# Later output products and spread v groups in the attention steps of a four-layer kernel

## The chip, the core and the metric

The kernel runs on one core of one Trainium2 chip. A core has TensorE (PE) for matrix products, VectorE (DVE), ScalarE (ACT) and GpSimd (POOL) for the rest, SyncE (SP), which here only issues transfers, and 16 DMA engines that carry the transfers. Each engine works through its own list of instructions in order and waits on semaphores for the others. The metric is the device time of one launch in microseconds (us), the median of several runs.

## What is computed

Two blocks are applied in turn, A, B, A, B, each behind a layer norm and added to its input x (2048 tokens of 576 channels; bf16 inputs, output within the tolerance of the reference).

```python
def _A_ref(x, wqkv, wo):            # attention: 32 heads of 18 channels
    W, dil = (8, 2)                 # each token looks at itself and 7 earlier ones, 2 apart
    q, k, v = ...                   # x @ wqkv
    ...
    logits = jnp.einsum('bhsd,bhswd->bhsw', q, kg) * scale
    attn = _softmax(logits, axis=-1)
    o = jnp.einsum('bhsw,bhswd->bhsd', attn, vg)
    return o @ wo

def _B_ref(x, w_in, w_sp, b_sp, w_out):   # gated MLP, 2304 + 2304 channels
    z = _gelu(jnp.einsum('bsd,df->bsf', x, w_in))
    z1, z2 = z[..., :Fh], _layernorm(z[..., Fh:])
    g = jnp.einsum('ts,bsf->btf', w_sp, z2) + b_sp[None, :, None]
    return jnp.einsum('bsf,fd->bsd', z1 * g, w_out)

x = x + _A_ref(_layernorm(x), A_wqkv, A_wo)
x = x + _B_ref(_layernorm(x), ...)
x = x + _A_ref(_layernorm(x), A_wqkv, A_wo)
x = x + _B_ref(_layernorm(x), ...)
```

## The kernel before

The change touches only `layer_A`, which is built twice: with `li == 0` (the first attention) and with `li == 2` (the second). The order of its instructions on every engine is written out by hand and kept as written.

The 2048 tokens are cut into two halves and each half into nine query tiles of 114 tokens (the last of a half has 112), `NT = 18` tiles t. A tile reads the keys and values of its own tokens and of the 14 before them, so 128 rows. Every tile takes two steps, s = 2t and s = 2t + 1, each for 16 of the 32 heads; there are `NST = 36` steps. Rows of the residual stream are handled in blocks of 128 tokens, i = 0 to 15.

A step issues, in this order: the score products of the next step (`L_mm`, line 444, into two large PSUM tiles of tag H) and their exponentials (`EXP`, line 453, on ScalarE, into one of four P buffers); then its own products with v (`PV`, line 464, TensorE), which VectorE normalises into the tile's buffer o_t (lines 470 and 471; there are three o_t buffers, so tile t + 3 overwrites tile t's). After the second step of a tile SP issues a transposing DMA from o_t to one of three slots (line 474). Then come the functions that a table holds for this step:

- `PG` (line 409): a group of q or k columns for 512 tokens, five products; VectorE evacuates it to a staging buffer (line 378), and SP and POOL issue transfers from there to the packed q/k tile QK. The groups of the second token half run inside the steps.
- `VW` (line 386): half of the v columns for one tile, five products, evacuated by VectorE or ScalarE into `v_ext`.
- `O_CP` (line 483): VectorE copies a transposed tile from its slot into a ring `oT` of five row blocks.
- `WO(i, hh)` (line 509): half of the output columns of row block i, five products from `oT`; VectorE adds the residual input `xo` (line 512) into `x_new`.
- `XO(i)`: SP loads the residual input of row blocks i and i + 1 (288 KB in the first attention).
- `LN_STATS(i)` on VectorE, then `LN_XN(i)` on POOL, the layer norm for the MLP that follows; `XST(i)`, SP's store of the new residual; `LN_T(i)`, SP's transposing DMA of the normalised block into `xnT`.
- `O_T`: the last two tiles are transposed on TensorE (line 489) instead of by DMA.
- `load_win2a`, `win2b_piece`: POOL issues loads of the MLP's weights.

`PV`, `PG`, `VW`, `WO` and `O_T` all take their PSUM tile from one set of four (tag PT), in turn. Transfers from SP are issued one after the other; each waits for its data to be ready before the next is issued.

Before the change, the step of `WO(i, 0)` follows from the tile t that completes row block i (`row_step`): 2t + 6 or 2t + 5, at the end 2t + 4 and 2t + 3; the second half runs one step later, so from step 8 on (first attention) or 7 on (second) there is about one half a step, with a gap in the middle, where the first token half ends, and two halves in step 32. The v groups of the second token half run from step 18 to 33 in the first attention, two steps for each tile.

After the steps the MLP follows. Its first products (line 815) are mixed with the last output products by the scheduler; the first thing it does on ScalarE after the gelus (line 829) is a square (line 833).

Of the kernel before, what the change touches and what calls it, by code (L numbers as in the profile page):

```python
# [18 lines left out]
P = 128  # L19
# [46 lines left out]
class K:  # L66
# [258 lines left out]
    def layer_A(self, li):  # L325
        nc, tc, cfg = self.nc, self.tc, self.cfg
        S, NT, XW, NS = cfg.S, cfg.NT, cfg.XW, cfg.NS
# [31 lines left out]
        def tdim(t):  # L359
            nq = cfg.tiles[t][1]  # L360
            return HALO + nq, nq

        def q0_(t):
            return cfg.tiles[t][0]
# [67 lines left out]
        NST = 2 * NT  # L432
# [101 lines left out]
        if li == 0:  # L534
# [114 lines left out]
            nvw0, nvw = 4, 9  # L649
        else:  # L650
# [12 lines left out]
            nvw0, nvw = 0, 4  # L663
# [14 lines left out]
        def at(s, f, *a):  # L678
            table.setdefault(s, []).append((f, a))
        pgs = [(d, qk, cc) for d, cc in ((0, 2), (1, 2), (2, 2), (0, 3), (1, 3), (2, 3), (3, 2), (3, 3), (4, 2), (4, 3))  # L680
               for qk in ((1, 0) if d < 4 else (0,))]
        PG_END = 14
        pre, pgs = pgs[:6], pgs[6:]
        for k_, (d, qk, cc) in enumerate(pgs):
            at(1 + k_ if li == 0 else (k_ * PG_END) // len(pgs), PG, d, qk, cc, True)
        for t in range(nvw, NT):
            for hh in range(2):
                if li == 0 and t == nvw:
                    at(13 * hh, VW, t, hh, True)
                else:  # L690
                    at(2 * t - 2 + hh, VW, t, hh, 2 * t - 2 + hh >= PG_END and hh == 0)
        row_step = {}
        for i in range(NS):
            t = next(t_ for t_ in range(NT) if q0_(t_) + tdim(t_)[1] >= (i + 1) * P)
            row_step[i] = 2 * t + (6 if li == 0 and t < 10 else 5 if t < NT - 4 else 4 if t < NT - 2 else 3)
        for t in range(NT - 2):
            if t < NT - 4:
                at(2 * t + (5 if li == 0 and t < 10 else 4), O_CP, t)
        for i in range(NS):
            s = row_step[i]  # L700
            if i % 2 == 0:
                at(max(s - 5, row_step[i - 3] + 1) if i >= 4 else s - 5, XO, i)
            at(s, WO, i, 0)
            at(s + 1, WO, i, 1)
            at(s + 1, LN_STATS, i)
            at(s + 2, LN_XN, i)
            at(s + 2, XST, i)
            if i < NS - 1:
                at(max(s + 4, 24 + (5 * i) // 4) if li == 0 else s + 4, LN_T, i)
        for t in range(NT - 4, NT - 2):  # L710
            at(2 * t + 3, O_CP, t)
        if li == 0:
            at(0, self.load_wo, nc.sync)
            for f in reversed(self.load_win2a(nc.gpsimd)):
# [368 lines left out]
```

## Time and profile before

| | |
|---|---|
| median of 3 runs | 1185.18 us (1184.57 to 1185.57) |
| the profiled execution | 1188.89 us, of which the profiled span is 1187.1 us |
| mean granted TensorE clock | 0.999 |

Busy time of the engines by stage, from the profile's windows (us; clock is the share of TensorE's full clock that was granted):

| stage | length | PE | DVE | ACT | POOL | clock |
|---|---|---|---|---|---|---|
| before the steps, first attention (0 to 41) | 41 | 38.28 | 33.91 | 20.31 | 24.01 | 1.00 |
| its steps 0 to 7 (41 to 64) | 23 | 22.30 | 16.93 | 17.53 | 13.54 | 1.00 |
| steps 8 to 13 (64 to 84) | 20 | 16.73 | 13.64 | 10.57 | 9.27 | 0.91 |
| steps 14 to 17 (84 to 92) | 8 | 7.52 | 7.01 | 6.98 | 7.62 | 1.00 |
| steps 18 to 33 (92 to 128) | 36 | 35.17 | 32.38 | 31.07 | 29.33 | 1.00 |
| last steps (128 to 135) | 7 | 6.44 | 6.20 | 3.39 | 6.04 | 1.00 |
| first MLP (135 to 620) | 485 | 481.81 | 200.82 | 118.95 | 77.77 | 1.00 |
| second attention and its MLP's start (620 to 760) | 140 | 136.52 | 101.98 | 103.78 | 96.54 | 1.00 |
| second MLP (760 to 1187) | 427 | 421.52 | 142.02 | 64.68 | 23.46 | 1.00 |

How to read the views shown below: the timeline gives the start of a merged run of instructions, its length, the engine, the line of the kernel, what it writes and reads, and in brackets how long the engine sat idle just before and whose event ended that. A list of waits gives the engine and line that waited, who ended the wait, the total, the count and the longest. A window gives its length, the busy time of PE, its weight loads, DVE, ACT and POOL (with counts), then the granted clock, the DMA share and GB/s. Matrix products are pipelined, so their shown lengths overlap; distances from start to start are used for their cost.

### The profile page before, as it was taken

How to read it: one execution, taken by the hardware profiler on the slowest of the kernel's cores; microseconds unless marked ns; L12 is line 12 of the kernel's file. 1: busy time of each engine (PE TensorE's matmuls, PEld its weight loads, DVE VectorE, ACT ScalarE, POOL GpSimd, SP SyncE). 2: the span in 40 equal slices, each digit the busy share in tenths (PEclk: the TensorE clock that was granted, in tenths of full speed). 3: DMA queues.
4: the chain of work that ended last, by engine and by line, in shares of the span. 5: the costliest groups of instructions: out<-in, count | busy, mean ns of one | idle time of the engine just before them, and what ended most of it. 6: DMA issues, size and time to landing. Idle time of an engine off the chain costs nothing. (4 is left out here: it accounts for less than half of the span.)

```text
span 1187.1 us, 20409 instructions
## 1 busy us (share of the span) xinstructions
PE 1166.3 (98%) x8307; PEld 622.3 (52%) x8406; DVE 554.9 (47%) x1232; ACT 377.3 (32%) x621; POOL 287.6 (24%) x383
## 2 busy tenths in 40 slices
PE   9989999999999999999999999999999999999998
PEld 5557544444444444457755774444444444444676
DVE  8778687332233232245556886863232233232321
ACT  5568677211100111102156786770111110111000
POOL 4758784100000000001143867840000000000000
PEclk9999999999999999999999999999999999999999
DMA  8989994000000000049656998900000000001332
GB/s 196 201 154 208 180 198 100 23 12 12 12 1 12 12 12 1 15 139 284 169 100 115 206 226 173 238 14 10 12 12 12 12 1 12 12 1 38 115 105 73
DMA packets 179478, 101.57 MB, mean 86 GB/s; under 512 B 135711, under 2 KB 160735, under 8 KB 179384
## 3 DMA queue, kind: packets, MB, share of 16 engines
q1 hardware_dynamic: 166520, 78.50, 31.3%
q0 software_dynamic: 6512, 16.00, 5.4%
q10 hardware_dynamic: 6352, 5.75, 1.6%
q8 instruction: 66, 1.08, 0.4%
q14 instruction: 28, 0.23, 0.1%
HBM read 42.39 MB, written 16.53 MB: 50 GB/s over the span
## 5 line engine op out<-in xcount | busy, mean ns | idle before, releaser
L929 PE MATMUL pg<-Wq,Z 128*128 128x512 bf16 x2258 | 497.8, 379 | 2.5
L929 PEld LDWEIGHTS <-Z 128*128 128x128 bf16 x2304 | 225.4, 98 | 271.8
L933 DVE TENSOR_TENSOR g_tmp<-pg,ln_xn 128x512 f32<-128x512 f32 x144 | 99.6, 692 | 422.5 <-PE pg L929 422.5
L924 ACT ACTIVATE z1T<-pz 128x1024 bf16<-128x1024 f32 x36 | 34.9, 1021 | 497.4 <-PE pz L905 493.8
L80 POOL DMA_DIRECT2D wout<-in_B_w_out_dram x4 | 4.3, 1065 | 600.8 <-PE pg L929 600.8
L971 PE MATMUL po<-wout,Z 128*128 128x288 bf16 x1152 | 141.4, 286 | 0.0
L453 ACT ACTIVATE P_sb<-L_ps 128x912 bf16<-128x912 f32 (+1 forms) x144 | 125.8, 929 | 42.3 <-PE L_ps L444 41.8
L971 PEld LDWEIGHTS <-Z 128*128 128x128 bf16 x1152 | 112.7, 98 | 28.8
L815 PEld LDWEIGHTS <-xnT 128*128 128x128 bf16 (+1 forms) x800 | 66.5, 97 | 83.7 <-issue 26.5
L815 PE MATMUL pz<-win2a,xnT 128*128 128x512 bf16 x380 | 103.9, 380 | 2.3 <-ACT zp L829 1.4
L934 DVE TENSOR_TENSOR Z<-g_tmp,z1T 128x512 bf16<-128x512 f32 x144 | 99.7, 692 | 12.6 <-DVE g_tmp L933 0.5
L905 PEld LDWEIGHTS <-w 128*128 128x128 bf16 (+1 forms) x640 | 53.7, 97 | 74.0 <-issue 13.6
L409 PE MATMUL pp<-xnT,wqk_sb 128*128 128x512 bf16 x341 | 82.3, 382 | 2.1 <-DVE o_t L471 0.6
L829 ACT ACTIVATE zp<-pz 128x1024 bf16<-128x1024 f32 x64 | 65.5, 1023 | 36.0 <-PE pz L815 16.9
L981 DVE TENSOR_TENSOR x_new<-po,xo 128x288 f32<-128x288 f32 (+1 forms) x64 | 28.8, 456 | 87.7 <-PE po L971 83.6
L905 PE MATMUL pz<-xnT,w 128*128 128x512 bf16 (+1 forms) x314 | 66.2, 380 | 0.3
L905 PE MATMUL pz1s<-xnT,w 128*128 128x512 bf16 (+1 forms) x312 | 65.3, 379 | 0.7 <-issue 0.6
L831 DVE CUSTOM_DVE_ANT_0 Z<-zp 128x1536 bf16<-128x1536 bf16 x32 | 56.8, 1774 | 12.5 <-ACT zp L829 7.6
L815 PE MATMUL pz<-win2b,xnT 64*128 64x512 bf16 (+1 forms) x240 | 59.7, 380 | 0.0
L80 POOL DMA_DIRECT2D QK<-stg x81 | 50.7, 631 | 35.6 <-DVE stg L378 18.7
L245 POOL TENSOR_SCALAR ln_xn<-x_new,ln_mv,ln_rstd 128x576 bf16<-128x576 f32 x23 | 53.0, 2306 | 2.0
L386 PE MATMUL pv<-wv_sb,xnT 128*128 128x288 bf16 (+1 forms) x360 | 52.8, 286 | 0.6 <-DVE o_t L471 0.5
(118 smaller groups left out, 1007.1 us busy)
## 6 DMA issues: line engine op xcount, KB each, us to landing
xres<-x_new SPq DMA_DIRECT2D x48, 288.0 KB
xo<-xres SPq DMA_DIRECT2D x32, 288.0 KB
wout<-in_B_w_out_dram POOLq DMA_DIRECT2D x4, 1296.0 KB, 8.6
xo<-xres SPq DMA_DIRECT2D x8, 576.0 KB
w<-in_B_w_in_dram SPq DMA_DIRECT2D x16, 256.0 KB
QK<-stg POOLq DMA_DIRECT2D x53, 72.0 KB, 4.7
QK<-stg SPq DMA_DIRECT2D x41, 72.0 KB
xo<-in_A_x_dram SPq DMA_DIRECT2D x8, 288.0 KB
```

The lines of the kernel that those rows point to most:

```text
L80: return eng.dma_start(out=out, in_=in_)
L245: e.tensor_scalar(out=xn[:nrows, 0:D], in0=x_t[:nrows, :], scalar1=mv[:nrows, 0:1], scalar2=rstd[:nrows, 0:1], op0=ALU.subtract, op1=ALU.mult)
L409: nc.tensor.matmul(pp[:, :], lhsT=w, rhs=self.xnT[:, c, PADL + cc * 512:PADL + (cc + 1) * 512], start=(c == 0), stop=(c == 4))
L453: nc.scalar.activation(out=P_bufs[(2 * s + jp) % 4][:nk, :, :, 0:nq], in_=Lv[:nk, :, :, 0:nq], func=ACT.Exp, scale=scale)
L815: nc.tensor.matmul(pzvs[ci][:, sub * 512:sub * 512 + w], lhsT=self.xnT[r0:r1, c, PADL + i * P:PADL + (i + 1) * P], rhs=win2(c)[r0:r1, c0 + ...
L829: nc.scalar.activation(out=zp[:, c0:c0 + cn], in_=pzvs[ci][:, 0:cn], func=ACT.Gelu_apprx_tanh, accum_out=sums[:, ci:ci + 1])
L831: nc.vector.tensor_tensor_reduce(out=spare[:, 0:SQ_D], in0=zp[:, 0:SQ_D], in1=zp[:, 0:SQ_D], scale=1.0, scalar=0.0, op0=ALU.mult, op1=ALU. ...
L905: nc.tensor.matmul(outs[a_], lhsT=w1[r0:r1, c, sub * P:(sub + 1) * P], rhs=self.xnT[r0:r1, c, PADL + q * 512:PADL + (q + 1) * 512], start= ...
L929: nc.tensor.matmul(pg[:, :], lhsT=Z[:, jj, i, sub * P:(sub + 1) * P], rhs=Wq[q][:, i, :], start=(i == 0), stop=(i == NS - 1))
L933: nc.vector.tensor_tensor(out=tmp[:], in0=pg[:, :], in1=bsp[:, qs], op=ALU.add)
L934: nc.vector.tensor_tensor(out=uT(jj)[:, sub, qs], in0=tmp[:], in1=z1Ts[jj, sub][:, qs], op=ALU.mult)
L971: nc.tensor.matmul(acc[hh], lhsT=uT(j // 2)[:, j % 2, i * P:(i + 1) * P], rhs=wouts[j // NJH][:, j % NJH, hh * 288:(hh + 1) * 288], start= ...
```

## The change

The table is filled by other rules. The output products get a hand-written list of steps, `wo_steps`. In the first attention row block i < 8 has its halves in steps 10 + 2i and 11 + 2i, then (26, 27), (28, 29), (30, 30), (31, 32), (33, 34), (34, 35), (35, 36), (37, 38). In the second it is 9 + 2i and 10 + 2i, then (25, 26), (27, 28), (29, 30), (31, 32), (33, 34), (34, 35), (35, 36), (37, 38). So the halves of the first row blocks run two steps later than before, those from block 8 on at the same step or one later, and step 32 has one half in place of two.

What hangs on a row block moves with it: `XO` (five steps before the first half), `LN_STATS`, `LN_XN`, `XST` and `LN_T`. `O_CP(t)` moves to step 2t + 6 at the latest (before: 2t + 5 for t < 10 in the first attention, else 2t + 4), or to the step before its row block's product. In the first attention the v groups of the second token half (tiles 10 to 17) spread over steps 14 to 32, four in five steps, in place of one in each of the steps 18 to 33; in the second they stay.

The built order on the engines shows it: on TensorE the products of line 509 leave the steps 8 and 9 and the v products stand in steps 14 to 17; on SP the first `XO` goes from before the q/k transfers of the second staging buffer to behind the transposing DMA of tile 2.

```diff
-        for t in range(nvw, NT):
-            for hh in range(2):
-                if li == 0 and t == nvw:
-                    at(13 * hh, VW, t, hh, True)
-                else:
-                    at(2 * t - 2 + hh, VW, t, hh, 2 * t - 2 + hh >= PG_END and hh == 0)
-        row_step = {}
+        vws = [(t, hh) for t in range(nvw, NT) for hh in range(2)]
+        if li == 0:
+            at(0, VW, *vws[0], True)
+            at(13, VW, *vws[1], True)
+            vws = vws[2:]
+        for k_, (t, hh) in enumerate(vws):
+            s = PG_END + (5 * k_) // 4 if li == 0 else 2 * t - 2 + hh
+            at(s, VW, t, hh, s >= PG_END and hh == 0)
+        lag = 10 if li == 0 else 9
+        wo_steps = [(lag + 2 * i, lag + 2 * i + 1) for i in range(8)]
+        wo_steps += ([(26, 27), (28, 29), (30, 30), (31, 32), (33, 34), (34, 35)] if li == 0 else
+                     [(25, 26), (27, 28), (29, 30), (31, 32), (33, 34), (34, 35)]) + [(NST - 1, NST), (NST + 1, NST + 2)]
+        for t in range(NT - 2):
+            s = wo_steps[q0_(t) // P][0] - 1
+            if t < NT - 3:
+                at(min(2 * t + 6, s), O_CP, t)
         for i in range(NS):
-            t = next(t_ for t_ in range(NT) if q0_(t_) + tdim(t_)[1] >= (i + 1) * P)
-            row_step[i] = 2 * t + (6 if li == 0 and t < 10 else 5 if t < NT - 4 else 4 if t < NT - 2 else 3)
-        for t in range(NT - 2):
-            if t < NT - 4:
-                at(2 * t + (5 if li == 0 and t < 10 else 4), O_CP, t)
-        for i in range(NS):
-            s = row_step[i]
+            s, s1 = wo_steps[i]
             if i % 2 == 0:
-                at(max(s - 5, row_step[i - 3] + 1) if i >= 4 else s - 5, XO, i)
+                at(max(s - 5, wo_steps[i - 3][1]) if i >= 4 else s - 5, XO, i)
             at(s, WO, i, 0)
-            at(s + 1, WO, i, 1)
-            at(s + 1, LN_STATS, i)
-            at(s + 2, LN_XN, i)
-            at(s + 2, XST, i)
+            at(s1, WO, i, 1)
+            at(s1, LN_STATS, i)
+            at(s1 + 1, LN_XN, i)
+            at(s1 + 1, XST, i)
             if i < NS - 1:
-                at(max(s + 4, 24 + (5 * i) // 4) if li == 0 else s + 4, LN_T, i)
-        for t in range(NT - 4, NT - 2):
-            at(2 * t + 3, O_CP, t)
+                at(max(s1 + 3, 24 + (5 * i) // 4) if li == 0 else s1 + 3, LN_T, i)
+        at(2 * (NT - 3) + 3, O_CP, NT - 3)
```

## The prediction

> **What bounds the kernel now.** I read the page first, then TensorE's waits in the two attentions, then the timelines of TensorE and VectorE step by step, then the granted clock by window. The page says who sets the time:
>
> ```profile
> PE 1166.3 (98%) x8307; PEld 622.3 (52%) x8406; DVE 554.9 (47%) x1232; ACT 377.3 (32%) x621; POOL 287.6 (24%) x383
> ```
>
> TensorE is busy for 98% of the span, so a reordering can win only what TensorE stands idle or runs slowly: 1187.1 - 1166.3 = 20.8 us of idle time, plus time at a lowered clock. TensorE's waits from 64 to 130 us (the first attention's steps 8 to 34), with total, count and longest:
>
> ```profile
> PE pw L509 <- DVE oT L483: 2.9, 2, 2.4
> PE L_ps L444 <- ACT P_sb L453: 0.9, 3, 0.4
> PE pp L409 <- DVE o_t L471: 0.6, 1, 0.6
> ```
>
> Most of it is one wait of an output product (L509) for VectorE's copy of a transposed tile into oT (L483). TensorE's timeline around it (start, us, what; in brackets the idle time before it):
>
> ```profile
> 69.48 0.57 PE L464 MATMUL O_ps<-v_ext,P_sb 128*128 128x19 bf16 x16
> 69.90 1.24 PE L409 MATMUL pp<-xnT,wqk_sb 128*128 128x512 bf16 x5
> 73.58 0.79 PE L509 MATMUL pw<-wo_sb,oT 128*128 128x288 bf16 x5 [2.45 <-DVE oT L483]
> ...
> 74.63 0.57 PE L464 MATMUL O_ps<-v_ext,P_sb 128*128 128x19 bf16 x16
> 75.75 0.61 PE L409 MATMUL pp<-xnT,wqk_sb 128*128 128x512 bf16 x1 [0.56 <-DVE o_t L471]
> 76.58 1.49 PE L409 MATMUL pp<-xnT,wqk_sb 128*128 128x512 bf16 x3 [0.22 <-issue]
> 77.86 1.32 PE L509 MATMUL pw<-wo_sb,oT 128*128 128x288 bf16 x5
> ...
> 79.45 0.57 PE L464 MATMUL O_ps<-v_ext,P_sb 128*128 128x19 bf16 x16
> ```
>
> Each step has one L464 group (PV), so the distance of two PV starts is a step's length. Step 9, whose PV starts at 66.94, takes 2.54 us. Steps 10 and 11, with the same work, take 5.15 and 4.82. VectorE shows the cause, and the granted clock shows a second loss:
>
> ```profile
> 68.64 0.69 DVE L378 CAST stg<-pp 128x512 bf16<-128x512 f32 x1 [0.26 <-PE pp L409]
> 73.19 0.34 DVE L483 COPY oT<-o_slot 128x570 bf16<-128x570 bf16 x1 [3.86 <-DMA o_slot<-o_t]
> ```
> ```profile
> 76.00:78.00 2.00, 1.78 (x5) 0.74 (x5) 1.28 (x4) 0.53 (x1) 1.41 (x3) 0.50 0.13 18
> ```
>
> The copy of tile 2 waits 3.86 us for its transposing DMA, issued on SP at 64.42. After the idle time TensorE runs at 0.50 of its clock (third number from the end), which the trace's clock record puts at 3.41 us long. The excess adds up: 2.45 + 0.56 + 0.22 idle, plus 3.41 / 2 = 1.71 lost at half clock, is 4.94; the two steps' excess over 2.53 each is 4.91.
>
> **The change, part by part.** Prices of TensorE's groups, from start to start: score products L 0.33 (64.08 to 64.41), PV 0.42, a q/k group (PG) 1.07, an output half (WO) 0.71, a v group (VW) 0.61 (92.17 to 92.78). Steps by kind, from PV starts: PG alone 2.09 (51.88 to 64.41 over six), PG+WO 2.53, WO alone 1.88 (84.24 to 91.75 over four), VW+WO 2.16 (91.75 to 104.72 over six). WO alone has 1.46 us of TensorE work in 1.88: there the exponentials (1.75 us of ScalarE a step) bind. No work is added or removed, so I sum step lengths.
>
> First attention, steps 8 to 34:
> - Steps 8 and 9 lose their output products: 2 x (2.09 - 2.53) = -0.88.
> - Steps 10 and 11 return to 2.53: -4.91, before what is left of the stall.
> - Steps 14 to 17 gain a v group: 4 x 2.16 against 7.51 measured: +1.13.
> - Steps 18, 23, 28 and 33 have none any more: 1.88 each against 2.17, 2.08, 2.25 and 2.28: -1.26.
> - Step 24 gains an output half (2.24 to 2.16), step 30 has two (2.25 to 2.78), step 32 one instead of two (2.78 to 2.16): -0.17.
> - Step 34 lasts 2.69 with 0.41 + 0.46 idle. The half that moves here needs no late tile and fills that: PV 0.42, two halves 1.42, transposes 0.25 make 2.09; two MLP matmuls (0.43) that stood there come later: -0.17.
>
> Sum -6.26. Against it stands what remains of the stall. The copy of tile 2 moves behind step 10, but the buffers of o_t number three: VectorE's write of o_t for tile 5, in step 10 too, overwrites what tile 2's transposing DMA reads, and waits for the same landing. So the wait on VectorE does not go; it starts later (about 68.9 us) and TensorE's cover grows. Behind it on VectorE queue the q/k evacuation, the copy and the first sum of step 10; TensorE waits for them through the four PSUM buffers of tag PT, first at step 11's q/k group, nominally 71.0 us. When the DMA lands therefore decides. In the trace 12 of its 16 increments came at 70.58 to 71.72, the last four at 73.12 to 73.16. Ahead of it on SP stood the first residual load (XO, 288 KB; its 256 packets fill 63 to 66 us). The change puts that load behind it, with SP issuing the transpose some 0.5 us earlier. I take the landing 2.2 us earlier, near 71.0: VectorE is free at 71.4, TensorE stalls 0.4 us, and VectorE's backlog (2.03 us of work a step in steps 13 to 19 against 2.16) costs perhaps 0.4 more: 0.8 in all. Bounds: 0 (landing at 70.5) and, with the landing unmoved, 2.6 us idle plus 1.71 at half clock.
>
> Where the stall goes, what is late next? The last q/k columns (d = 4) are evacuated at step 12, about 77.6 us, and issued by SP until 81.1; POOL's moves of this kind land in a median of 4.9 us, so near 86; step 18 reads them near 86.7. No wait, within 1 us. The residual load now lands near 72.5, when VectorE is about there. At the end SP is busy almost without a gap from 117.7 to 144.6, row 12's sums come a step later, and the first square of the MLP waits 2.45 us for a transpose, which costs TensorE 0.88: I give back 0.5 (0 to 1). First attention: -6.26 + 0.8 + 0.5 = -5.0.
>
> Second attention, the same output products, its v groups unmoved:
>
> ```profile
> 686.56 0.57 PE L464 MATMUL O_ps<-v_ext,P_sb 128*128 128x19 bf16 x16
> ...
> 688.67 0.56 PE L464 MATMUL O_ps<-v_ext,P_sb 128*128 128x19 bf16 x16
> ...
> 690.62 0.56 PE L464 MATMUL O_ps<-v_ext,P_sb 128*128 128x19 bf16 x16
> ...
> 713.16 0.79 PE L509 MATMUL pw<-wo_sb,oT 128*128 128x288 bf16 x5 [0.48 <-DVE oT L483]
> ```
>
> Steps 23 and 24 have no output product, yet last 2.11 and 1.95 us with 1.36 us of work: two free places, filled by the change (+0.05 and +0.21). They come from steps 7 and 8, where PG, VW and WO together are TensorE's own 3.15 us; without WO 2.43, above ScalarE's 1.75 + 0.41: -1.44. Step 32 loses its second half (2.77 to 2.16): -0.61. Step 34 (here 0.42 + 0.48 idle) as above: -0.2. Sum -2.0; the row tail on POOL (about 3.1 us a row, back to back at the end) gives back 0.4 (0 to 0.8): -1.6. The moved residual loads, stores and transposes keep their distance in steps to what reads them, and SP's own waits in this attention are for VectorE and POOL.
>
> Total -6.6. Against the profiled execution's own span: 1187.1 to 1180.5, and its time of 1188.89 lies 1.79 outside the span. That execution is 3.71 above the median of 1185.18; the difference is applied to the median: 1178.6.
>
> The trace has half clock after 2.45 and 0.56 us of idle time with work between. The Trainium skill, "TensorE: Matmul & The Clock Gate", section "What's actually happening", says that the clock halves after an idle window of about 3.4 us; read so, neither gap would have done it, and the 1.71 would not belong to the stall, for a total of -4.9 and 1180.3. The measured half clock decides here.
>
> The residual load is moved behind the transpose, yet the trace shows POOL's q/k moves on the same transfer engines at that time. The Trainium skill, "DMA: Bandwidth & Descriptors", section "Issuing engines are not separate DMA queues", says that transfers interleave on the same 16 engines whoever started them; that speaks against the earlier landing, and with an unmoved landing the sum is that of the second case below.
>
> **The rivals.**
> 1. *Forecast*: as above. Its own range: nothing given back and a small 0.5 us further is -8.8, 1176.4; 2.0 of stall and both tails at their full price is -6.26 + 2.0 + 1.0 - 2.0 + 0.8 = -4.5, 1180.7.
> 2. *The transpose lands at 73.2 as before*, since the last four increments came 1.4 us after the twelfth and may have nothing to do with the load. Then 4.3 replaces 0.8: -6.6 + 3.5 = -3.1, 1182.1. For it: the o_t write waits for it just the same. Against: a 288 KB load leaves its front.
> 3. *The end holds the MLP*: SP's queue, nearly full from 117.7, does not come earlier, the square waits as late as before, and the first attention's gain becomes its wait. Only the second's 1.6 stays: 1183.6. Against: before 105 us SP has room, and its transposes are tied to steps.
> 4. *Slower*: the transpose of tile 3, now behind the residual load and four q/k moves, holds VectorE in step 12 (o_t of tile 6 waits for it). TensorE's cover ends near 77.1 us; each microsecond later costs one, and the half clock 1.71. It eats the whole gain when it lands after 77.1 + 6.6 - 1.7 = 82.0, and is slower by 0.2% from 84.4 on; at 85.5, 1188.7 - 1185.2 = 3.5 slower. Against: it landed at 73.9 before, 4.5 us after its issue, and the slowest in that stretch took 8.7.
>
> That the instructions do not move is excluded: the built order shows the output products gone from steps 8 and 9 and the v groups in 14 to 17.
>
> **How the numbers follow.** About 0.2% (2.4 us) is what a measurement of this kernel tells from no change. Chances: forecast 0.68, landing unmoved 0.19, held end 0.06, slower 0.04, a gain beyond 8.8 us 0.03. The second case straddles 1182.8: four fifths of it is faster. Faster 0.68 + 0.15 + 0.03 = 0.86; same 0.04 + 0.06 = 0.10; slower 0.04. The time is the forecast's, 1178.6; the range 1176.4 to 1182.6 holds cases one and most of two, about 0.83.
>
> **What would show it.** Right: steps 8 and 9 at 2.1 us, steps 10 to 12 near 2.5 with under 1 us idle and a clock of 1.00; VectorE's wait at o_t (L471) instead of the copy, ending near 71; steps 14 to 17 near 2.16; no idle before L509 in step 34; in the second attention steps 7 and 8 at 2.4, 23 and 24 at 2.2. Wrong: a clock of 0.50 near 72 to 80, a wait of VectorE until 73, a longer idle time before the first gelus, or spread steps well above 2.16.

## The result, and the profile after

| | before | after |
|---|---|---|
| median | 1186.05 us (1183.72 to 1190.33, 22 runs) | 1183.52 us (1181.44 to 1187.09, 22 runs) |
| ratio of the times | | 0.9975, 95% interval 0.9966 to 0.9985 |
| the profiled execution, its span | 1188.89, 1187.1 us | 1182.29, 1180.5 us |

The medians differ by 2.5 us; the ratio is worth 3.0 us, with an interval of 1.8 to 4.0. Forecast were 6.6 us and 1178.6; the time is 0.9 us above the range. The two profiled executions do differ by the forecast 6.6 us. That agreement is chance, and the trap of this case: the profile of before is of an execution 2.8 us above the median of the 22.

The line of engines on the page of after, then TensorE's waits from 64 to 130 us (total, count, longest):

```profile
PE 1169.8 (99%) x8406; PEld 622.2 (53%) x8406; DVE 553.0 (47%) x1232; ACT 377.3 (32%) x621; POOL 285.8 (24%) x383
```
```profile
PE L_ps L444 <- ACT P_sb L453: 1.3, 4, 0.4
PE pv L386 <- DVE o_t L471: 1.0, 2, 0.7
PE pw L509 <- DVE x_new L512: 0.2, 1, 0.2
```

The 2.9 us at the output product are gone. TensorE's PV groups (the lines between them are left out) and one line of VectorE at the place of the old stall (start, length, engine and line; idle time and its end in brackets), then two windows (the clock is the third number from the end):

```profile
67.99 0.56 PE L464 MATMUL O_ps<-v_ext,P_sb 128*128 128x19 bf16 x16
70.52 0.57 PE L464 MATMUL O_ps<-v_ext,P_sb 128*128 128x19 bf16 x16
73.06 0.57 PE L464 MATMUL O_ps<-v_ext,P_sb 128*128 128x19 bf16 x16
75.59 0.57 PE L464 MATMUL O_ps<-v_ext,P_sb 128*128 128x19 bf16 x16
...
70.35 0.46 DVE L471 TENSOR_TENSOR o_t<-O_ps,rec 128x288 bf16<-128x288 f32 x1 [1.50 <-DMA o_slot<-o_t]
```
```profile
74.00:76.00 2.00, 2.00 (x41) 1.24 (x40) 1.90 (x8) 1.22 (x3) 0.58 (x1) 1.00 1.03 174
76.00:78.00 2.00, 2.00 (x39) 1.47 (x36) 1.97 (x8) 1.68 (x3) 1.63 (x4) 1.00 0.76 211
```

Steps 10 to 12 last 2.53 us each, at full clock. VectorE waits at the write of o_t instead of at the copy, until 70.35, and TensorE does not notice. This is the picture that the prediction drew. The first row blocks of the MLP tell another part, on ScalarE and TensorE:

```profile
137.61 0.84 ACT L835 ACTIVATE Z<-zp 128x768 bf16<-128x768 bf16 x1 [2.55 <-DMA xnT<-stg]
...
139.60 0.81 PE L817 MATMUL pz<-win2a,xnT 128*128 128x512 bf16 x3 [0.98 <-ACT zp L831]
```

The square waits 2.55 us for transposes out of the staging buffers, and TensorE loses 0.98 behind it. In the second attention the free places are filled, steps 23 and 24 (forecast 2.2 each; PV groups alone):

```profile
677.22 0.56 PE L464 MATMUL O_ps<-v_ext,P_sb 128*128 128x19 bf16 x16
679.33 0.56 PE L464 MATMUL O_ps<-v_ext,P_sb 128*128 128x19 bf16 x16
681.54 0.57 PE L464 MATMUL O_ps<-v_ext,P_sb 128*128 128x19 bf16 x16
```

### The profile page after: what moved, and what is told of

It reads as the page before. It is cut to its first block, busy times and chain, and to the rows that moved or that the text cites. A ratio compares the mean times of both kernels' runs of the same rounds, so it can differ in the third digit from the quotient of the medians.

```text
span 1180.5 us, 20534 instructions
## 1 busy us (share of the span) xinstructions
PE 1169.8 (99%) x8406; PEld 622.2 (53%) x8406; DVE 553.0 (47%) x1232; ACT 377.3 (32%) x621; POOL 285.8 (24%) x383
## 4 chain that ended last, share of the span: by engine, by line
PE 89%; POOL 4%; DMA 2%; DVE 2%; issue 1%; ACT 1%; SPq 0%; POOLq 0%; ACTq 0%; DVEq 0%
PE pg L931 42%; PE po L973 12%; PE pz L817 9%; PE pz L907 6%; PE pz1s L907 6%; PE pp L409 4%; PE pv L386 2%; PE O_ps L464 2%; PE L_ps L444 2%; POOL ln_xn L245 2%; PE pw L509 2%; PE pzs L817 1%; DMA o_slot<-o_t 1%; DMA QK<-win2a 1%; POOL QK L80 1%
## 5 line engine op out<-in xcount | busy, mean ns | idle before, releaser
L817 PE MATMUL pz<-win2b,xnT 128*128 128x512 bf16 (+1 forms) x256 | 65.7, 380 | 0.0
```

The source lines that it names most:

```text
L817: nc.tensor.matmul(pzvs[ci][:, sub * 512:sub * 512 + w], lhsT=self.xnT[r0:r1, c, PADL + i * P:PADL + (i + 1) * P], rhs=win2(c)[r0:r1, c0 + ...
```

## The experiments

All ratios are against runs of the kernel before on the same chip; the chips differ between groups of experiments, so across groups the ratios are compared, not the medians. Besides the time, three lengths are read from each profile: the steps of an attention from their PV starts, and the stretch from the last PV of the first attention to the first PV of the second ("between"), which holds the first MLP.

**One half of the change at a time, and the kernel before again.** `first_only` and `second_only` fill the table by the new rules in one attention and by the old ones in the other; `b_again` is the kernel before; `xo0_later` is the kernel before with the first residual load two steps later.

```diff
+        if li == 0:
...
+        else:
...
```

The new rules stand in the first branch and the old in the second; in second_only the condition is `li == 2`. The edit of xo0_later:

```diff
-                at(max(s - 5, row_step[i - 3] + 1) if i >= 4 else s - 5, XO, i)
+                at(max(s - 5, row_step[i - 3] + 1) if i >= 4 else s - 5 + (2 if li == 0 and i == 0 else 0), XO, i)
```

> The kernel before, unchanged, for a second profile. Theory A (the execution profiled before the prediction had an unusually late landing of tile 2's transposing DMA): steps 10 and 11 together last 5.1 to 8 us here instead of 9.97, the span is 1182 to 1186 instead of 1187.1. Theory B (every execution has that stall; what the change wins there it loses somewhere in most executions): steps 10 and 11 last 9.5 to 10.5 us again, with the half clock, whatever the span. Against the kernel before: ratio 1.000 within 0.002.

> Only the first attention has the new table, the second is as before. The prediction's term is -5.0 us (ratio 0.9958). Theory A: the usual stall is smaller than the recorded one by the 3 to 4 us by which the recorded execution lies above the median, so -1 to -2 us (0.9983 to 0.9992). Theory B: the same ratio, but with steps 10 and 11 of the kernel before long in every profile, and a loss that shows outside of the steps.

> Only the second attention has the new table, the first is as before. The prediction's term is -1.6 us (0.9986); the profile of the changed kernel has its 36 steps 2.9 us shorter. Theory A: this part is steady, -1.6 to -2.9 us (0.9976 to 0.9986), most of the change's measured gain. Theory B: -0.5 us or less, the gain being given back at the start of the MLP.

> The kernel before, with one edit: the first residual load of the first attention is issued two steps later, behind the transposing DMA of tile 2. If that load is what makes the transpose land late: VectorE's wait before the copy of tile 2 falls from 3.86 us to under 2, steps 10 and 11 together last under 7 us, and the time falls by 1 us or so in the median. If the landing has another cause: the wait stays between 2 and 4 us and the time is the same within 1 us.

| | median (us) | ratio to before, 95% interval | span | steps 10 to 12 | 2 to 34, first | 0 to 34, second | between |
|---|---|---|---|---|---|---|---|
| before (its profile) | | | 1187.1 | 12.50 | 77.86 | 82.97 | 501.33 |
| b_again | 1187.43 | 0.9989 (0.997 to 1.0008) | 1184.2 | 7.66 | 72.93 | 84.45 | 500.26 |
| first_only | 1186.85 | 0.9994 (0.9976 to 1.0013) | 1184.3 | 7.60 | 72.71 | 83.77 | 502.19 |
| second_only | 1184.64 | 0.997 (0.9954 to 0.9986) | 1183.3 | 7.61 | 72.90 | 81.75 | 501.51 |
| xo0_later | 1188.16 | 1.0007 (0.9989 to 1.0026) | 1183.4 | 8.35 | 74.67 | 82.95 | 500.83 |
| after | 1183.52 | 0.9975 (0.9966 to 0.9985) | 1180.5 | 7.60 | 74.08 | 80.09 | 501.91 |

b_again settles the first question. The same kernel, and TensorE's steps 9 to 11 show no stall (PV groups alone, then VectorE's copy of tile 2):

```profile
68.00 0.57 PE L464 MATMUL O_ps<-v_ext,P_sb 128*128 128x19 bf16 x16
70.53 0.57 PE L464 MATMUL O_ps<-v_ext,P_sb 128*128 128x19 bf16 x16
73.07 0.57 PE L464 MATMUL O_ps<-v_ext,P_sb 128*128 128x19 bf16 x16
75.66 0.56 PE L464 MATMUL O_ps<-v_ext,P_sb 128*128 128x19 bf16 x16
...
70.96 0.34 DVE L483 COPY oT<-o_slot 128x570 bf16<-128x570 bf16 x1 [0.57 <-DMA o_slot<-o_t]
```

So 4.8 of the 4.9 us do not belong to every execution. Without the stall the first attention's part gains 0.2 us in its steps (72.93 to 72.71), and the stretch that follows is longer by 0.7 to 1.9. By the ratios the second attention's part has all of the measured gain; the interval of first_only, down to 0.9976, leaves room for 2.9 us. xo0_later does not make the median faster, but it does not decide on the load: VectorE does not wait for the transpose there, and instead its sum of step 8 waits for the load that now comes later, so that steps 9 to 11 are long all the same:

```profile
70.11 0.46 DVE L512 TENSOR_TENSOR x_new<-pw,xo 128x288 f32<-128x288 f32 x1 [3.23 <-DMA xo<-in_A_x_dram]
```

**How often the stall comes.** Three more profiles of the old table in the first attention, one of them (`before_sp`, below) with another edit far from it, and one more of after.

> The kernel before, one more profile, to see how often steps 10 and 11 stall. Theory A (in about half of the executions): either a stall of 1.5 to 5.5 us there or none. Theory B (rare, one execution in ten): none.

> As the look before it, a further profile of the kernel before: theory A expects a stall at steps 8 to 11 in about half of such profiles, theory B in one of ten.

> The changed kernel once more, for a second profiled execution. Theory A (the 4.9 us of steps 10 and 11 were a late landing of one execution, and the change's gain in the median is 2.9 us of steps in the second attention, nothing in the first): steps 10 to 12 at 2.5 us each, the second attention's 36 steps at 80.1, the first's 2 to 34 at 72.5 to 73.0 unless a late landing falls into them; median 2.5 to 3.5 us under that of before. Theory B (the change removes a stall that most executions have): the same steps, but a median 5 us or more under that of before on this chip.

before_look1 and before_look2 have steps 10 to 12 at 8.06 and 8.00 (0.4 too long). before_sp has them at 13.11; VectorE and TensorE there repeat the profile of before almost to the number (3.86 and 2.45):

```profile
73.84 0.34 DVE L483 COPY oT<-o_slot 128x570 bf16<-128x570 bf16 x1 [3.73 <-DMA o_slot<-o_t]
...
74.24 0.79 PE L509 MATMUL pw<-wo_sb,oT 128*128 128x288 bf16 x5 [2.31 <-DVE oT L483]
```

Of seven profiles with the old table, steps 8 to 12 are too long by 4.9 and 5.5 us in two, by 0.4 in two and by nothing in two; the seventh, xo0_later, has 1.8 from the moved load. Of the eleven with the new table none has more than 0.2 there. So the change does remove this stall; large it is in two profiles of seven, which are too few to say in what share of the executions. after_again: 1183.9 us, 0.9973 (0.9957 to 0.9988), steps 10 to 12 at 2.5 each, 2 to 34 in 72.52 us, between 502.45: theory A's numbers, except for the second attention with 81.20 (step 34 lasts 2.80 us there, 1.89 in after).

The new table has stalls elsewhere. In `first_row12_sp` (below) step 21 lasts 6.51 us, since VectorE's write of o_t, which the three buffers bind to a transposing DMA, waits as the prediction said it could, and a v group behind it:

```profile
96.00 0.46 DVE L471 TENSOR_TENSOR o_t<-O_ps,rec 128x288 bf16<-128x288 f32 x1 [2.63 <-DMA o_slot<-o_t]
...
96.51 1.38 PE L386 MATMUL pv<-wv_sb,xnT 128*128 128x288 bf16 x5 [2.91 <-DVE o_t L471]
```

**The spread v groups.** `wo_only` has the new steps of the output products in both attentions and the old places of the v groups. `v_block` is the changed kernel with one v group in each of the steps 14 to 29, so that the four free steps are neighbours.

```diff
-            s = PG_END + (5 * k_) // 4 if li == 0 else 2 * t - 2 + hh
+            s = PG_END + k_ if li == 0 else 2 * t - 2 + hh
```

> The later output products in both attentions, the v groups left where they were. Theory A (a step that loses its v group alone between steps that keep theirs gains almost nothing, because its score products wait for the exponentials of the step before; four steps that gain one pay in full): steps 14 to 17 sum to 7.5 us in place of 8.7, steps 18, 23, 28 and 33 last 2.1 to 2.3 as with the spread groups, and the first attention's 36 steps take about 75.4 us in place of 76.4 (both without a stall). The start of the first MLP takes most of that back (TensorE's wait for ScalarE there 1.2 to 2 us in place of 1.0), so the time is within 1 us of the changed kernel, ratio about 0.997. Theory B (the prediction's prices: a step without a v group lasts 1.88): the free steps are worth as much as the four added groups cost, and the first attention's steps take 76.4 us or more.

> The changed kernel, but the v groups of the first attention stand one in each of the steps 14 to 29, so that the four steps without one (30 to 33) are neighbours. Theory A (only neighbouring free steps gain): steps 14 to 29 last 2.16 each, 31 to 33 about 1.9 to 2.1 and 30, with two output halves, 2.2, against 2.67, 2.49, 2.98 and 2.28 (30 to 33) in the changed kernel; steps 14 to 33 together about 0.7 to 1.0 us shorter than in the changed kernel (44.5 to 44.9). Theory B (the late steps last longer because VectorE, POOL or SP are loaded there, not for where the free steps stand): steps 30 to 33 stay above 2.2 each and the sum stays within 0.3 us. The time is within 1 us of the changed kernel's under either, since the start of the MLP may take the gain.

wo_only: 1182.96 us, ratio 0.9968 (0.9952 to 0.9984). Steps 14 to 17 sum to 7.51 as both theories had it (after: 8.73). Its first attention took 82.64 us from PV 0 on, and so does not test the 75.4: another transfer was late in step 1, which lasts 6.36 us (TensorE stood 3.04 us, the clock fell to 0.50 meanwhile, and it ran on at that clock), and steps 18 to 33 hold 1.6 us more than in wo_row12 below.

```profile
52.51 2.29 PE L409 MATMUL pp<-xnT,wqk_sb 128*128 128x512 bf16 x5 [3.04 <-DMA xnT<-ln_xn]
```
```profile
50.00:52.00 2.00, 0.00 (x0) 0.00 (x0) 0.26 (x1) 0.19 (x1) 0.00 (x0) 0.50 0.77 124
```

v_block: 1185.07 us, ratio 0.9994 (0.9976 to 1.0012). Steps 18 to 33 sum to 34.38, against 35.22 to 35.52 with the spread table in first_only, after_again, row12 and row12_sp: neighbouring free steps gain 0.8 to 1.1 us, the sum that theory A gave. Not each step is as it said: 30 and 33 are short (2.25 and 1.62, against 2.68 and 2.28 in after_again), 31 and 32 last 2.21 and 2.31. (The expected 44.5 to 44.9 for steps 14 to 33 had been set against after, whose 45.61 holds some 1.4 us of other waits; measured are 43.11.) The time does not show it. In the profile TensorE comes to the copy of tile 15 before its transposing DMA has landed, and step 34 lasts 6.00 us:

```profile
129.45 0.34 DVE L483 COPY oT<-o_slot 128x570 bf16<-128x570 bf16 x1 [1.98 <-DMA o_slot<-o_t]
...
129.85 1.38 PE L509 MATMUL pw<-wo_sb,oT 128*128 128x288 bf16 x5 [3.15 <-DVE oT L483]
```

Whether that is so in most of its executions is not known from one profile. What binds a lone free step is seen in after, step 18:

```profile
87.70 0.37 PE L444 MATMUL L_ps<-QK 32*128 32x114 bf16 x8
88.45 0.38 PE L444 MATMUL L_ps<-QK 32*128 32x114 bf16 x8 [0.38 <-ACT P_sb L453]
```

The second half of the score products waits until ScalarE has emptied its PSUM tile; the step ends at 2.18 us, not at 1.88. The four steps of which 1.88 is the mean show it too, in the profile of before: 14 to 17 last 2.13, 1.66, 2.16 and 1.56, the first of them hardly less than a step with a v group (2.16).

**What holds the MLP's start.** `row12` is the changed kernel with row block 12 normalised into a small buffer, so that the staging buffers are read out one row block earlier. `wo_row12` is wo_only with the same edit.

```diff
-            if li == 0 and 4 <= i < 4 + 3 * NSTG:
+            if li == 0 and 4 <= i < 12:
```

> The changed kernel, but row block 12 of the first attention is normalised into one of the small buffers of blocks 0 to 3 and 13 to 15 instead of the q/k staging buffer. Theory A (the first MLP's start is held because its first square writes where the staging buffer lies and so waits for the transpose of row block 12, which the change puts a step later): the square's wait falls from 2.55 us to 0.5 to 1.0, TensorE's wait for ScalarE behind it from 0.98 to under 0.2, the stretch between the two attentions from 501.9-502.2 to 500.9-501.3 us, the time to about 1 us under the changed kernel's, ratio 0.9965. Theory B (the square is held by ScalarE's or POOL's own work, or the wait is only run-to-run variation): TensorE's wait stays at 0.8 to 1.3 us and the time at the changed kernel's, ratio 0.9975.

> The later output products in both attentions, the v groups where they were, and row block 12 in a small buffer: the version that theory A points to. Theory A: the first attention's steps take 75.4 us, and what they gain is not taken back at the MLP's start (TensorE's wait for ScalarE there under 0.4 us): time 1.5 to 2.2 us under the changed kernel's, ratio about 0.9958. Theory B: no better than the changed kernel, ratio 0.9975.

row12: 1184.26 us, 0.9984 (0.9967 to 1.0002); between 502.40: the time of theory B. ScalarE shows that the mechanism was theory A's all the same, and TensorE that the wait has only moved:

```profile
135.59 0.84 ACT L835 ACTIVATE Z<-zp 128x768 bf16<-128x768 bf16 x1 [0.49 <-DMA xnT<-stg]
...
149.29 0.81 PE L817 MATMUL pz<-win2a,xnT 128*128 128x512 bf16 x3 [1.36 <-ACT zp L831]
```

The square starts 2.0 us earlier (137.61 before the edit), TensorE's wait behind it is gone, and 10 us later there is one of 1.36. POOL, VectorE and ScalarE ahead of it:

```profile
143.90 0.64 POOL L80 DMA_DIRECT2D ln_xn<-in_B_b_sp_dram  x1 [3.18 <-DMA xnT<-ln_xn]
144.57 0.58 POOL L848 TENSOR_TENSOR z_rstd<-z_rstd,neg_half 128x1 f32<-128x1 f32 x1
...
145.19 0.81 DVE L858 TENSOR_SCALAR Z<-zp,z_mean,z_rstd 128x2048 bf16<-128x2048 bf16 x1 [7.00 <-POOL z_rstd L848]
...
148.13 1.02 ACT L831 ACTIVATE zp<-pz 128x1024 bf16<-128x1024 f32 x1 [2.79 <-DVE z_sq L844]
```

A load of b_sp, which reuses the memory of the normalised rows, stands in POOL's queue and waits 3.18 us for the last row's transpose. Behind it queues the small z_rstd of the MLP's first row block, so VectorE and POOL normalise that block late, and ScalarE's gelu of a later block finds its buffer (there are three) still in use.

wo_row12: 1183.0 us, 0.9963 (0.9947 to 0.9979); TensorE's wait there 0.95, between 501.98; its steps 0 to 34 take 76.73, not 75.4: steps 0 and 1 take 4.53 (3.71 in b_again), and steps 18 to 33, with one output half more than before, 35.94 (35.23).

The next kernels also take the b_sp load out of POOL's queue, in both MLPs: `wo_row12_sp`, `row12_sp` (the changed kernel with both edits), `before_sp` (the kernel before with this edit alone), and `first_row12_sp` (first_only with both edits).

```diff
-                self.dma(bsp, self.B_b_sp.partition_broadcast(P), eng=nc.gpsimd)
+                self.dma(bsp, self.B_b_sp.partition_broadcast(P), eng=nc.sync)
```

> The version with the later output products in both attentions, v groups where they were, row block 12 in a small buffer; and the load of b_sp, which stands in POOL's queue behind the last layer norm and waits there 3.18 us for the last transpose, is issued by SP instead (in both MLPs). Theory A (with the square freed, POOL's queue is the next thing that holds the MLP's start): POOL's z_rstd comes about 3 us earlier against the last layer norm, TensorE's wait for ScalarE near 147 to 149 us falls from 0.95-1.39 to under 0.2, the stretch between the attentions from 502.0 to about 501.0 us, the time about 1 us under that version's, ratio 0.9955. Theory B (yet another holder, such as the sixteen transposes or the last row's layer norm itself): the wait stays at about 1 us or moves again, ratio 0.9963.

> The changed kernel with both holders taken away: row block 12 in a small buffer and the load of b_sp issued by SP. Against the version with the v groups left where they were it isolates the spreading. Theory A: steps 14 to 17 sum to 8.7 us and 18 to 33 to 35.2 (against 7.5 and 35.9), so the spreading costs 0.4 to 0.6 us; TensorE's wait for ScalarE at the MLP's start under 0.3 us; ratio 0.996 to 0.9965. Theory B (the prediction's 1.88 for a free step): 18 to 33 sum to 34.2 or less and the spreading costs nothing.

> The kernel before, with only the load of b_sp moved from POOL's queue to SP's. Theory A (the hold matters only where the steps end earlier; before, TensorE is held at the MLP's start by 0 to 0.9 us): the same within 0.5 us, ratio 0.9995 to 1.000. Theory B (POOL's wait holds the MLP's start whatever the steps do): about 1 us faster, ratio 0.999 or less, and a stretch between the attentions at 500.3 us or less.

> The change in the first attention alone, with row block 12 in a small buffer and the load of b_sp issued by SP; the second attention as before. Theory A (the first attention does gain, by the stall that it removes from some executions, and the MLP's start took it back): 1 to 2 us under the kernel before with the b_sp load moved (0.9986), so ratio 0.997 to 0.998, the stretch between the attentions near 500.9 us. Theory B (the first attention's part brings nothing in itself): ratio 0.9985 or more.

> The changed kernel with both holders taken away, once more. Theory A: the ratio stays at 0.9945 to 0.9960, the stretch between the attentions at 500.8 to 501.2 us, steps 10 to 12 at 2.5 each. Theory B (the six runs were a lucky draw): ratio 0.9970 or more.

| | median (us) | ratio to before, 95% interval | between | last PV of the second attention to the end |
|---|---|---|---|---|
| wo_row12_sp | 1182.3 | 0.9958 (0.9942 to 0.9974) | 501.43 | 472.39 |
| row12_sp | 1181.6 | 0.9947 (0.993 to 0.9964) | 500.87 | 472.38 |
| row12_sp_again | 1182.27 | 0.996 (0.9943 to 0.9977) | 500.87 | 472.46 |
| before_sp | 1185.08 | 0.9986 (0.9971 to 1.0) | 500.28 | 471.77 |
| first_row12_sp | 1185.04 | 0.9972 (0.9957 to 0.9987) | 500.78 | 471.83 |

In row12_sp POOL's z_rstd follows the last layer norm at once, and TensorE has no listed wait from 127 to 165 us. POOL first, then TensorE at the place where row12 lost 1.36:

```profile
137.87 2.29 POOL L245 TENSOR_SCALAR ln_xn<-x_new,ln_mv,ln_rstd 128x576 bf16<-128x576 f32 x1
140.22 0.24 POOL L248 COPY ln_xn<-ln_xn 128x64 bf16<-128x64 bf16 x1
140.42 0.56 POOL L848 TENSOR_TENSOR z_rstd<-z_rstd,neg_half 128x1 f32<-128x1 f32 x1
...
147.55 0.27 PE L817 MATMUL pzs<-win2b,xnT 128*128 128x256 bf16 x1
147.66 0.81 PE L817 MATMUL pz<-win2a,xnT 128*128 128x512 bf16 x3
```

The stretch between the attentions falls by 1.3 us, from 502.18 (mean of after, after_again and first_only) to 500.87, and the stretch behind the second attention by 0.8 (473.14 and 473.24 in after and after_again). The first attention's part may now show in the time: first_row12_sp is at 0.9972, before_sp at 0.9986. The two stand against different runs of before and their intervals overlap, so this step is not shown. before_sp missed theory A's 0.9995; 1.3 of its 1.7 us lie behind the second attention (473.06 to 471.77), which the expectation had left out. row12_sp has the lowest times, 1.5 to 3.3 us under the changed kernel by the ratios (0.9947 and 0.996 against 0.9975 and 0.9973, of 1186; the intervals of the nearer two overlap). Some of that belongs to the b_sp load alone, which is worth 1.7 us without the change (before_sp); the changed kernel with that edit alone was not run. In wo_row12_sp the stretch is 501.43 and not the expected 501.0, though TensorE has no listed wait there either. That spreading the v groups costs 0.4 to 0.6 us shows in the steps (14 to 33 take 43.54 in wo_row12, 43.95 and 44.03 in row12 and row12_sp), but not in the time: row12_sp and wo_row12_sp are within each other's interval.

## Why the prediction failed, point by point

**The step that failed** is "Steps 10 and 11 return to 2.53: -4.91", together with "the difference is applied to the median". The stall, its cause and its removal were read rightly: VectorE's copy waited for tile 2's transposing DMA, the wait moved to the o_t write and ended at 70.35 (forecast near 71), and the clock stayed full. But the 4.91 us were booked for every execution, while the profiled execution lay 3.71 us above the median of three, as the prediction itself noted. The stall is large in two of seven profiles with the old table; the mean over the six other than xo0_later is (4.9 + 5.5 + 0.4 + 0.4) / 6 = 1.9 us, and the middle two have 0.4 each. That the residual load ahead of it made the landing late is not borne out either. From the issue of tile 2's transposing DMA on SP to the start of what waits for it on VectorE it takes 8.8 us in before (64.42 to 73.19), but 6.0 in b_again (64.92 to 70.96) and 6.3 in before_look2 (64.68 to 70.94), with the load still ahead, and 6.6 in after (63.75 to 70.35), with the load behind. The 20.8 us of idle time that the prediction starts from are too many as well: 99 of TensorE's 8406 products are missing from that profile (x8307 beside x8406 weight loads); after, with all of them, has 10.7.

**The give-back at the MLP's start** was right as a mechanism and mis-sized: 0.5 us taken, 1.3 measured. The stretch between the attentions has a mean of 500.89 in six profiles with the old table (before, b_again, second_only, xo0_later, before_look1 and before_look2) and 502.18 with the new one. TensorE's waits for ScalarE there explain 0.82 of it (1.24 on the mean in after, after_again and first_only, 0.42 in the six), the two MLP matmuls that left step 34 0.43. The prediction had listed "a longer idle time before the first gelus" as a sign against it; the wait came behind them. Row block 12's last half runs in step 34 in place of 33, and the square writes where its staging buffer lies.

**The free steps.** Steps 18, 23, 28 and 33 were to last 1.88 each (-1.26). They last 2.17, 2.07, 2.06 and 2.28 in row12_sp_again, 8.58 in place of 8.78: -0.2. The 1.88 was a mean over four neighbouring free steps. A single one waits for ScalarE, as the lone score product above shows; in v_block, where they are neighbours, the gain is there in the sum.

**What held.** Steps 8 and 9: -0.88 forecast, 5.06 to 4.18 measured. Steps 14 to 17: +1.13, 7.52 to 8.73 is +1.21. Steps 24, 30 and 32: -0.17, 7.27 to 7.08 in row12_sp_again is -0.19 (in after they take 7.73, since step 32 lasts 2.98 there). Second attention: steps 7 and 8 -1.44 forecast, 6.30 to 5.07 is -1.23 (2.53 each, not 2.43); 23 and 24 +0.26, 4.06 to 4.32; 32 and 33 together 5.05 to 4.49, -0.56, where -0.61 was forecast for 32. Step 34 gains 0.8 in the first attention (2.69 to 1.90) where 0.2 was taken: its idle 0.9 us is filled. In the second it lasts 1.9 in five of ten profiles with the new table and 2.1 to 2.8 in the others (2.7 to 3.4 with the old). The give-back of 0.4 in the second attention did not come: 473.06 to 473.14 to the end.

Put together without the stall of steps 10 and 11: second attention 83.43 to 80.74 (means of eight and ten profiles), -2.7; first attention's steps -0.2, the MLP's start +1.3; sum -1.6. What is left to the measured -2.5 to -3.2 (the medians here, 0.9973 of 1187.18 for after_again) is 0.9 to 1.6 us. With the waits as they fell into the profiles, steps 2 to 34 of the first attention take 74.80 on the mean of the seven with the old table and 73.51 on the mean of seven with the new one (without v_block and the three with the v groups unmoved): -1.3 in place of -0.2, which makes the sum -2.7. These profiles reach from 72.5 to 78.4, so the difference of the means is known to about 1 us only, and the profiled executions without the large stall mostly lie under their kernel's median (1185.97 against 1187.43 in b_again).

That the large stall fills the gap is therefore argued, not shown, and one record speaks against it. The time lost at half clock, (1 - clock) times the span averaged over the runs, is 0.4 us in after and 0.8 in after_again, and 1.7 to 2.4 in the runs of before (clock to three places, so each run's is known to 0.6 us); first_only with 1.5 and second_only with 1.3, against 2.4 for before beside them, each have a share of that. But both profiles with the large stall also have half clock, and on the chip of after_again the executions recorded at a clock of 1.000, few as they are, differ as much as all: 1186.57 (median of four) and 1183.47 (median of eight). Where the rest of the gain comes from stays open.

**The rivals.** The third, the end that holds the MLP, forecast 1183.6 with a chance of 0.06, and the time is 1183.5. Its mechanism is near the one found, but its sum is near by luck: it booked the whole removal of the stall against the wait, where the stall is mostly absent and the wait smaller. The unmoved landing (1182.1) does not hold in the profile of after, with 70.35, and in the kernel before 73.2 is itself no rule; the slower case, tile 3 late, does not occur: steps 12 and 13 last 2.53 and 2.26.

The prediction weighed the Trainium skill, "TensorE: Matmul & The Clock Gate", section "What's actually happening", against the half clock of that stall. The sum by the page, 1180.3, erred in the same way, since it kept the stall itself.

## What to carry to other kernels

A stall at a late transfer, seen in one profile that lies above the median, is a chance and not a price: profile the same kernel again before it is booked, or weigh it by how far that execution stands from the median. Where steps are bound now by one engine and now by another, a place is worth what its neighbours leave it, and a mean over a run of free steps does not price a single one. When the end of a stage is moved, look through every queue for what stands behind the last rows: here a square, then a load in POOL's queue, each held the next stage. With the first taken away the wait moved and the time did not fall (0.9984); with both it fell (0.9947 and 0.996).

## What the runs showed of the hardware

The same transposing DMA lands at different times in different executions: VectorE's copy of tile 2, which waits for it, started at 70.96 in b_again, 70.94 in before_look2, 73.19 in the profile of before and 73.84 in before_sp; that is 6.0, 6.3, 8.8 and 8.8 us after its issue on SP. Other steps stall in other profiles (1, 21 and 34 in the versions above). What makes the transfers late is open.

Half clock comes in stretches of 3.41 us (six in these 18 profiles, by the trace's clock record, start and end of the kernel left out) or 6.83 us (four), and at times behind small gaps alone. In b_again the clock is halved from 686.2 to 689.6 us, behind a listed wait of 0.32 us:

```profile
683.45 0.38 PE L444 MATMUL L_ps<-QK 32*128 32x114 bf16 x8 [0.32 <-ACT P_sb L453]
```
```profile
684.00:686.00 2.00, 1.85 (x46) 1.28 (x43) 1.17 (x4) 2.00 (x3) 1.95 (x2) 1.00 1.29 194
686.00:688.00 2.00, 2.00 (x20) 1.27 (x17) 1.35 (x3) 1.50 (x3) 1.37 (x3) 0.54 1.99 310
```

and from 710 on behind waits of 0.42 and 0.91 within 2 us, while the same two waits in first_only left the clock full. The length agrees with the window of 3413 ns that the Trainium skill gives ("TensorE: Matmul & The Clock Gate", section "What's actually happening"). A whole idle window ahead of the half clock, as the page has it, was in none of the ten: in the 3.41 us before each, TensorE was idle for 0.46 us (b_again, 686) to 2.67 us (first_row12_sp, 96).
